# Reordering the opening of an attention-plus-Fourier kernel, and who copies its sums out of PSUM

## The chip, the cores and the metric

The kernel runs on one core of one Trainium2 chip. A core has a matrix engine (TensorE, "PE" in the profile; its weight loads are listed apart as "PEld"), a vector engine (VectorE, "DVE"), an activation engine (ScalarE, "ACT"), a general engine (GpSimd, "POOL") and a queue engine (SyncE, "SP"). Each runs its own list of instructions strictly in order and waits at semaphores for the others. Matrix results appear in PSUM, eight banks of 128 x 512 float32; operands lie in SBUF. DMA transfers are issued by an instruction on one of the engines' queues (here SP, ACT or POOL).

The metric is the device time of one execution in microseconds, the median of several runs. Less is better.

## The reference

Inputs are one sequence of 2048 rows of width 512 and fixed weights. What is computed, in float32:

```python
x = A_x                                                   # 1 x 2048 x 512
g = sigmoid((x * gate_w).sum(-1, keepdims=True))
qkv = x @ wqkv                                            # 32 heads of 16
p = softmax(q @ k.T * 16 ** -0.5)                         # per head, 2048 x 2048
a = (p @ v) @ wo
b = dft_seq_re @ (x @ dft_hid_re.T) - dft_seq_im @ (x @ dft_hid_im.T)
out = g * a + (1 - g) * b
```

`wqkv` and `wo` are scaled by 64, so the scores are large and the softmax needs the maximum of each row of scores subtracted.

## The kernel before

**Arithmetic.** TensorE takes rounded float32 operands ("F32R"). To keep precision, an operand is split into a rounded high part and the remainder: `split` (L369) is a copy on ScalarE (L370) and a subtraction on another engine (L371). A product is then three products: high x high, high x low, low x high.

**Two stages.** The program has a *front* and then *rounds*. The front computes q and k transposed (`project_t`, L432), v and the two hidden transforms (`project_s`, L464), and, beside them, a part of the *scans*. A scan is a first pass over the scores of two heads that finds each row's maximum. The rounds then do the scores proper, their exponentials on ScalarE, the sums of exponentials times values (`pv`, L671), the remaining scans, and the large sequence transform as filling (`fill`, L925).

**Slots in the front.** `products` (L351) issues one output tile: 12 pairs of operands, each as two half-height matmuls, one on the upper 64 rows of the array (L356) and, 17 pairs later, one on the lower 64 rows (`follow`, L340). 80 such tiles make 960 pairs. One pair is one *slot*: after each, `beside()` (L287) advances the counter `slots`, runs whatever `after(n, f)` (L263) made due n slots later, and, once `scan_at(FOLD_PACE)` has been called, issues scans at a spacing of 2.05 slots (`scan_folded`, L178). Each engine's program is the order in which these calls are made. Tile n uses PSUM bank n mod 3; `close` (L436) of tile n, run 28 slots after the tile's first slot, empties it by a ScalarE copy (L445, `eh`) and a VectorE subtraction (L446, `el`) and, for the first two groups of k, another ScalarE copy (L448). The parts are then stored to DRAM from SyncE's queue (L458).

**The start.** SyncE loads, in pieces, the transposed x (four column parts c, four row parts d, into `raws[0..3]`), and the columns of `wqkv` for q and k (`rq`, `rk`), each in a `near` and a `far` half. Meanwhile TensorE does `NWARM` transposes of an identity (L505). The splits of x part 0 and of the near half of `wq` are made at once, the others at slots given in L509 to L514. Tiles follow the `order` of L515: q and k of group 0 and q of group 1 for part 0, then k and q of group 0 for parts 1 to 3, then the other groups of q, then k.

**Scans in the front.** There are 64 scans for each pair p of heads, 368 (`FRONT`) in the front: pairs 0 to 4 and 48 scans of pair 5. In the front a scan handles folded keys: for each scan one ScalarE instruction (L190) reads one bank and one VectorE instruction (L192) another. The rows of q and folded keys for a pair are four tiles (`PARTS`: k0, k1, q0, q1) of four loads each, issued by `load_scan_beside` (L277), for pair 0 on SyncE's queue, for the others on ScalarE's. Twelve SBUF slots of 128 x 1024 (`stk0` to `stk11`), taken as a ring by `piece` (L102), hold raw weights, raw x and all such row tiles. Near the end of the front the rows for the rounds are loaded too: `used[0]` (28 loads) and `first_rows` (12 loads), both in one go on SyncE's queue.

**Folding the keys.** `fold_keys` (L416) takes a difference of two parts of k on GpSimd, splits it and stores it to `kf_d`; it is started 3 slots after the odd part's tile is closed.

**Quotients.** In the rounds the sums of exponentials times values of two heads and two halves of 1024 queries share one PSUM tile, `pvb`. After every 16 steps `quotients` (L705) copies `pvb` to SBUF tile `ob`. From macro round 42 on (`SINGLES`) ScalarE copies columns 0 to 255 (L710) and VectorE columns 256 to 511 (L711) of the same tile. The order of scores, scans and filling in a round is a table (`ORDERS`, L47); banks are chosen by a planner (`Banks`, L612) at build time.

## Time and profile before

| | |
|---|---|
| median of 3 runs | 1731.57 us (1730.52 to 1739.37) |
| profiled execution, its own time | 1734.79 us |
| its span, first to last instruction | 1732.8 us |
| mean granted TensorE clock | 0.994 |
| PE busy | 1708.2 us (99%) |
| DVE busy | 1249.2 us (72%) |
| ACT busy | 1358.7 us (78%) |
| POOL busy | 687.7 us (40%) |
| front, first product to last scan | 5.8 to 344.0 us |
| scans outside the front | 351.6 to 1595.5 us |

Times in profile rows count from the span's start. A row of the table of stretches has the stretch, its length, then busy time and number of instructions of each engine (of one source line alone where the text says so), the granted clock, the DMA engines' share and GB/s. A row of the timeline has start, duration, engine, line, operation, tiles and shapes; in brackets stands how long the engine was idle before and what ended that. A row of waits has who waited for whom, the sum in us, how often, and the longest. PE is counted busy where its pipeline still holds a matmul, so that small stalls show as a lower count of matmuls in a stretch and not as idle time.

### The profile page before, as it was taken

The page shows a single profiled execution, that of the slowest core. Times are in us where ns is not written, and L with a number is a line of the kernel's source. Part 1 is how long each engine was busy: PE and PEld are TensorE (multiplying, and loading weights), DVE is VectorE, ACT ScalarE, POOL GpSimd, SP SyncE. Part 2 cuts the span into 40 slices and gives each one's busy share as a digit, 9 for nine tenths or more (in the row PEclk, how much of TensorE's full clock was granted, in tenths as well). Part 3 has the DMA queues.
Part 4 walks back from the last instruction along what each step waited for, and adds up shares of the span by engine and source line. Part 5 has one row for each costly group of instructions (what it writes and reads, how often), then busy time and mean ns, then how long its engine had stood idle before and what let it go on. Part 6 is the DMA issues. An engine that isn't in the chain of part 4 may idle for free.

```text
span 1732.8 us, 36968 instructions
## 1 busy us (share of the span) xinstructions
PE 1708.2 (99%) x13657; PEld 1026.9 (59%) x13657; DVE 1249.2 (72%) x2385; ACT 1358.7 (78%) x2615; POOL 687.7 (40%) x860
## 2 busy tenths in 40 slices
PE   8999999999999999999999999999999999999998
PEld 6777778744435555555555555555555555555554
DVE  5589899866667777777777777777777777777434
ACT  5589988789997777777777777777777777777785
POOL 0254301344564544444444434434443443443121
PEclk9999999999999999999999999999999999999999
DMA  7575233564443333232333257333332422425522
GB/s 262 198 234 170 72 117 121 185 188 131 112 149 94 94 87 90 80 102 70 88 83 95 64 155 229 102 89 103 97 87 82 126 78 76 122 82 154 147 55 100
DMA packets 140004, 206.59 MB, mean 119 GB/s; under 512 B 58848, under 2 KB 61392, under 8 KB 139824
## 3 DMA queue, kind: packets, MB, share of 16 engines
q1 hardware_dynamic: 94992, 167.46, 31.5%
q0 software_dynamic: 41056, 27.86, 6.1%
q10 hardware_dynamic: 3776, 8.92, 1.9%
q8 instruction: 107, 1.75, 0.4%
q14 instruction: 73, 0.60, 0.1%
HBM read 137.89 MB, written 65.81 MB: 118 GB/s over the span
## 4 chain that ended last, share of the span: by engine, by line
PE 88%; DMA 4%; POOL 2%; issue 2%; DVE 1%; ACT 1%; SPq 0%; ACTq 0%; DVEq 0%; POOLq 0%
PE pvb L675 25%; PE z L920 21%; PE s L696 15%; PE s L665 12%; PE xy L340 5%; PE s L186 5%; PE xy L356 4%; DMA bs_d<-ol 1%; DMA o_d<-ol 1%; DMA wraw<-wqkv 0%; POOL ol L964 0%; ACT fold L190 0%; DVE y L865 0%; POOL el L275 0%; DMA lc<-ob 0%
## 5 line engine op out<-in xcount | busy, mean ns | idle before, releaser
L655 ACT ACTIVATE e<-s 128x512 f32<-128x512 f32 x2048 | 1073.4, 648 | 256.6 <-PE s L665 224.7
L698 DVE TENSOR_REDUCE mx<-s 128x1 f32<-128x512 f32 x1312 | 850.6, 687 | 284.3 <-PE s L665 194.9
L665 PE MATMUL s<-qs,ks 50*128 50x512 f32 x2048 | 656.7, 423 | 0.0
L675 PE MATMUL pvb<-e,va 128*17 128x512 f32 x4096 | 497.9, 596 | 0.0
L696 PE MATMUL s<-ks,qs 48*128 48x512 f32 x1312 | 487.9, 419 | 1.8 <-DVE mx L698 1.4
L920 PE MATMUL z<-b,chi 64*128 64x512 f32 x2060 | 471.9, 392 | 0.0
L665 PEld LDWEIGHTS s<-qs,ks 50*128 50x128 f32 x2048 | 338.7, 184 | 133.9 <-ACT e L655 110.4
L696 PEld LDWEIGHTS s<-ks,qs 48*128 48x128 f32 x1312 | 218.1, 185 | 197.4 <-issue 116.5
L920 PE MATMUL z<-b,clo 64*128 64x512 f32 x1030 | 300.9, 392 | 0.0
L920 PEld LDWEIGHTS z<-b,chi 64*128 64x128 f32 x2060 | 281.7, 186 | 27.4 <-issue 0.8
L192 DVE CUSTOM_DVE_ANT_0 fold<-s,fold 128x512 f32<-128x512 f32 x368 | 242.7, 689 | 32.9 <-ACT fold L190 14.2
L186 PE MATMUL s<-ks,qs 48*128 48x512 f32 x736 | 237.8, 404 | 5.6 <-ACT fold L190 5.3
L244 POOL CAST chi<-craw 128x512 fp32r<-128x512 f32 x126 | 77.3, 613 | 385.8 <-PE z L920 377.2
L190 ACT ACTIVATE fold<-s 128x512 f32<-128x512 f32 x368 | 203.1, 604 | 33.5 <-PE s L186 29.1
L675 PEld LDWEIGHTS pvb<-e,va 128*17 128x17 f32 x4096 | 90.1, 96 | 213.4 <-issue 212.2
L245 POOL TENSOR_TENSOR clo<-craw,chi 128x512 fp32r<-128x512 f32 x126 | 161.8, 1284 | 10.5
L920 PEld LDWEIGHTS z<-b,clo 64*128 64x128 f32 x1030 | 157.1, 186 | 13.6
L186 PEld LDWEIGHTS s<-ks,qs 48*128 48x128 f32 x736 | 135.8, 186 | 43.8 <-ACT fold L190 17.0
L714 POOL DMA_DIRECT2D lc<-ob x124 | 63.1, 515 | 230.1 <-DVE ob L711 211.0
L356 PE MATMUL xy<-w,b 64*128 64x512 f32 x384 | 121.9, 402 | 0.0
L340 PE MATMUL xy<-w,b 64*128 64x512 f32 x384 | 117.9, 395 | 0.0
L865 DVE SCALAR_TENSOR_TENSOR y<-z,g,y 128x512 f32<-128x512 f32 x44 | 32.5, 750 | 64.6 <-PE z L920 63.0
(130 smaller groups left out, 1509.5 us busy)
## 6 DMA issues: line engine op xcount, KB each, us to landing
craw<-cr SPq DMA_DIRECT2D x64, 256.0 KB
craw<-ci SPq DMA_DIRECT2D x64, 256.0 KB
qs<-q_d SPq DMA_DIRECT2D x110, 128.0 KB
ks<-k_d SPq DMA_DIRECT2D x108, 128.0 KB
ab_d<-ab SPq DMA_DIRECT2D x32, 256.0 KB
y_d<-y SPq DMA_DIRECT2D x32, 256.0 KB
b<-bs_d SPq DMA_DIRECT2D x32, 256.0 KB
o_d<-oh POOLq DMA_DIRECT2D x28, 256.0 KB, 9.6
```

Source lines behind the costliest of these rows:

```text
L186: nc.tensor.matmul(ps, rows.q[qb // 8][b:b + 48, qb % 8 * P:(qb % 8 + 1) * P], rows.k[c // 2][b:b + 48, c % 2 * 512:(c % 2 + 1) * 512], st ...
L190: seen_by(nc.scalar.activation(fold[j], ps, AF.Relu))
L192: seen_by(nc.vector.tensor_tensor_reduce(out=fold[j], in0=ps, in1=fold[j], scale=1.0, scalar=-3.0e38, op0=ALU.add, op1=ALU.max, accum_out= ...
L245: sub(lo, raw, hi.bitcast(F32))
L340: ins = nc.tensor.matmul(ps, lhs[64:P], rhs[64:P], start=False, stop=last)
L356: nc.tensor.matmul(ps, lhs[0:64], rhs[0:64], start=n == 0, stop=False)
L655: nc.scalar.activation(e, ps, AF.Exp, scale=SCALE)
L665: nc.tensor.matmul(ps, rows.k[kb // 8][b:b + 50, kb % 8 * P:(kb % 8 + 1) * P], rows.q[h][b:b + 50, c * 512:c * 512 + 512], start=True, sto ...
L675: nc.tensor.matmul(pvb[r:r + VC, :], va[:, kb, 2 * p + j, :], es[step][c, j][0], start=kb == 0, stop=kb == NB - 1, tile_position=(0, r))
L696: nc.tensor.matmul(ps, rows.q[qb // 8][b:b + 48, qb % 8 * P:(qb % 8 + 1) * P], rows.k[c // 2][b:b + 48, c % 2 * 512:(c % 2 + 1) * 512], st ...
L698: nc.vector.tensor_reduce(mx[p][:, j, qb, c:c + 1], ps, axis=AX.X, op=ALU.max)
L920: nc.tensor.matmul(ps, pr_.lhs(j), pr_.rhs(j), start=group.count[j] == 1, stop=group.count[j] == group.size)
```

## The change

Two groups of edits.

In the front:

- `NWARM` goes from 20 to 32 transposes, and three further groups of six transposes (`fillers`) are put after the third, sixth and ninth pair of the first tile.
- The slots at which operands are split move: x parts 1, 2 and 3 start at slots 10, 32 and 56 (before 18, 42 and 66); the far half of `wq` at 84 (before 52), the far half of `wk` at 124 with a spacing of 6 (before 76 with 4).
- The first `fold_keys` is started 36 slots after its tile is closed (before 3).
- The row tiles of pair 0 are loaded through GpSimd's queue (before SyncE's); those of the other pairs through SyncE's (before ScalarE's), beginning at scan 10 of pair 0 and scan 4 of the others (before 28 and 8), 5 slots apart (before 3).
- `used[0]` is loaded from scan 284 on, 5 slots between loads (before all at scan 312), and `first_rows` from scan 324 on, 3 slots between loads (before all at scan 334), into SBUF slots that are written out in `LAST_SLOTS` instead of the ring's next ones.

In the rounds:

- `quotients` copies all of `pvb` by one ScalarE instruction.

```diff
--- before.py
+++ after.py
@@ -35,10 +35,11 @@
 FRONT = 5 * SCANS + 48
 FOLDED = range(FRONT)
 FOLD_PACE = 2.05
-NWARM = 20
+NWARM = 32
 STEPS = NP * PERIODS
 MACROS = STEPS // 2
 LAG = 17
+LAST_SLOTS = ((6, 7, 0, 1), (8, 9, 10))
 SINGLES = 42
 EARLY = 0
 SPECTRAL = 8
@@ -94,14 +95,14 @@
 
 
         scanned, used, owner, next_slot = {}, {}, [None] * 12, [0]
-        HS = S // 2
+        HS, fixed = S // 2, []
 
         def free_slots():
             return [i for i in range(12) if owner[i] is None]
 
         def piece(dtype, name, who=None, ring=True):
 
-            i = next_slot[0] if ring else free_slots()[0]
+            i = fixed.pop(0) if fixed else next_slot[0] if ring else free_slots()[0]
             if ring:
                 next_slot[0] = (i + 1) % 12
             owner[i] = who
@@ -246,7 +247,7 @@
                 parts.append((hi, lo))
 
         seen, slots, due, count = [0], [0], [], [0]
-        first_rows = []
+        first_rows = Rows()
         pace = [None, 0.0]
         with ExitStack() as px:
             psf = px.enter_context(tc.tile_pool(name="psf", bufs=1, space=PSUM, reuse_waits="tile"))
@@ -277,9 +278,9 @@
             def load_scan_beside(p):
                 rows, loads = scanned.setdefault(p, Rows()), []
                 for part in PARTS:
-                    load_part(rows, None, p, part, nc.scalar if p else nc.sync, kf_d, True, loads.append)
+                    load_part(rows, None, p, part, nc.sync if p else nc.gpsimd, kf_d, True, loads.append)
                 for n, load in enumerate(loads):
-                    after((3 if p else 2) * n, load)
+                    after((5 if p else 2) * n, load)
 
             def scan_at(spacing):
                 pace[0] = spacing
@@ -294,17 +295,18 @@
                 while seen[0] < FRONT and pace[1] >= 1.0:
                     pace[1] -= 1.0
                     n = seen[0]
-                    if n % SCANS == (28 if n < SCANS else 8) and n - n % SCANS + SCANS < FRONT:
+                    if n % SCANS == (10 if n < SCANS else 4) and n - n % SCANS + SCANS < FRONT:
                         load_scan_beside(n // SCANS + 1)
-                    if n == FRONT - SCANS + 8:
-                        used[0] = Rows()
+                    if n in (FRONT - SCANS - 20, FRONT - SCANS + 20):
+                        loads = []
+                        fixed[:] = LAST_SLOTS[n > FRONT - SCANS]
                         for part in PARTS:
-                            load_part(used[0], "use", 0, part, nc.sync, k_d, True)
-                    if n == FRONT - SCANS + 30:
-                        first_rows.append(Rows())
-                        for part in PARTS:
-                            if part != "q0" or FRONT % SCANS < SCANS // 2:
-                                load_part(first_rows[0], "scan", FRONT // SCANS, part, nc.sync, k_d, True)
+                            if n < FRONT - SCANS:
+                                load_part(used.setdefault(0, Rows()), "use", 0, part, nc.sync, k_d, True, loads.append)
+                            elif part != "q0" or FRONT % SCANS < SCANS // 2:
+                                load_part(first_rows, "scan", FRONT // SCANS, part, nc.sync, k_d, True, loads.append)
+                        for k, load in enumerate(loads):
+                            after((5 if n < FRONT - SCANS else 3) * k, load)
                     scan_folded(n, 0, scan_bank)
                     done = behind(n - 1)
                     seen[0] += 1
@@ -346,7 +348,7 @@
                 if last:
                     close(ps)
 
-            starts = set()
+            starts, fillers = set(), []
 
             def products(parts, close):
 
@@ -364,6 +366,8 @@
                     behind_.append((ps, lhs, rhs, n == len(pairs) - 1, close))
                     if len(behind_) > LAG:
                         follow()
+                    if n % 3 == 2 and fillers:
+                        fillers.pop()(6)
                     beside()
 
             def split(hi, lo, raw, engine):
@@ -450,7 +454,7 @@
                             after(5, nc.gpsimd.tensor_copy, hi, s)
                             after(6, nc.gpsimd.tensor_sub, lo, s, hi.bitcast(F32))
                         if folded and c % 2:
-                            after(3, fold_keys, f, c - 1, even[0], s)
+                            after(36 if early and c == 1 else 3, fold_keys, f, c - 1, even[0], s)
                         after(9 if early else 12, store, 0, hi)
                         after(12 if early else 18, store, 1, lo)
 
@@ -501,17 +505,21 @@
                 after(40, nc.sync.dma_start, gb, gate.to_broadcast([P, D]))
 
                 warm = [scan_bank(), scan_bank()]
-                for n in range(NWARM):
-                    nc.tensor.transpose(warm[n % 2][:, 0:P], ident, ident)
+                def keep_warm(k):
+                    for n in range(k):
+                        nc.tensor.transpose(warm[n % 2][:, 0:P], ident, ident)
+
+                keep_warm(NWARM)
+                fillers.extend([keep_warm] * 3)
                 for d in range(ND):
                     split_x(d, 0)
                     split_w(wq, d, rq[d], cols=near)
                 for d in range(ND):
                     after(1 + 2 * d, split_w, wk, d, rk[d], nc.vector, near)
-                    after(52 + 4 * d, split_w, wq, d, rq[d], nc.vector, far)
-                    after(76 + 4 * d, split_w, wk, d, rk[d], nc.vector, far)
-                    for c in range(1, NC):
-                        after(24 * c - 6 + 4 * d, split_x, d, c)
+                    after(84 + 4 * d, split_w, wq, d, rq[d], nc.vector, far)
+                    after(124 + 6 * d, split_w, wk, d, rk[d], nc.vector, far)
+                    for c, at in zip(range(1, NC), (10, 32, 56)):
+                        after(at + 4 * d, split_x, d, c)
                 order = [(wq, q_d, 0, 0), (wk, k_d, 0, 0), (wq, q_d, 1, 0)]
                 order += [(w, dst, 0, c) for c in range(1, NC) for w, dst in ((wk, k_d), (wq, q_d))]
                 for n, (w, dst, f, c) in enumerate(order):
@@ -585,7 +593,7 @@
                 run_due(True)
 
         assert seen[0] == FRONT, seen
-        scanned[FRONT // SCANS] = first_rows[0]
+        scanned[FRONT // SCANS] = first_rows
 
         with ExitStack() as pa:
             psl = pa.enter_context(tc.tile_pool(name="psl", bufs=1, space=PSUM, reuse_waits="tile"))
@@ -707,8 +715,7 @@
                 if now[0] < SINGLES:
                     nc.vector.tensor_copy(ob, pvb)
                 else:
-                    nc.scalar.copy(ob[:, 0:256], pvb[:, 0:256])
-                    nc.vector.tensor_copy(ob[:, 256:512], pvb[:, 256:512])
+                    nc.scalar.copy(ob, pvb)
                 lc = sm.tile([P, 16], F32, tag="lc", name="lc")
                 for n, (c, j, r) in enumerate(quads):
                     nc.gpsimd.dma_start(lc[32 * n:32 * n + 32, :],
```

## The prediction

> **What bounds the kernel now.** The page comes first: how much of the span is TensorE's, and what the chain that ended last consists of.
>
> ```profile
> span 1732.8 us, 36968 instructions
> PE 88%; DMA 4%; POOL 2%; issue 2%; DVE 1%; ACT 1%; SPq 0%; ACTq 0%; DVEq 0%; POOLq 0%
> ```
>
> 88% of the chain is TensorE. So a time is won only where TensorE stands still or runs slowly, and 4% DMA and 2% "issue" in the chain say that such places exist. To find them I count products of the front (L356, one per slot) in stretches between the starts of output tiles. Columns: stretch, length, PE busy (count), PEld busy (count), granted clock, DMA share, GB/s.
>
> ```profile
> 5.81:16.43 10.62, 9.38 (x24) 6.42 (x25) 0.68 0.99 344
> 16.43:41.35 24.92, 21.26 (x85) 14.79 (x84) 1.00 0.66 243
> 48.07:50.95 2.88, 2.88 (x12) 2.14 (x13) 1.00 0.84 314
> 41.35:64.91 23.56, 21.05 (x85) 14.96 (x84) 1.00 0.74 255
> 90.23:102.86 12.63, 8.81 (x25) 4.94 (x24) 0.86 0.75 231
> 205.05:312.60 107.55, 95.44 (x301) 52.90 (x300) 1.00 0.34 106
> 312.60:324.74 12.14, 8.64 (x24) 5.20 (x25) 0.86 0.70 217
> ```
>
> A count one above a multiple of 12 is a product that only reaches into the stretch. Without scans a quiet tile takes 2.88 us, 0.240 us a slot (third row). With scans beside it, the long quiet stretch gives 107.55 / 300 = 0.3585 us a slot (sixth row). What the other rows have above these paces is what a better order could win:
>
> - 5.81 to 16.43: 10.62 - 24 x 0.240 = 4.86 us
> - 16.43 to 41.35: 24.92 - 84 x 0.240 = 4.76 us
> - 41.35 to 64.91: 23.56 - 84 x 0.240 = 3.40 us
> - 90.23 to 102.86: 12.63 - 24 x 0.3585 = 4.03 us
> - 312.60 to 324.74: 12.14 - 24 x 0.3585 = 3.54 us
>
> That is 20.6 us. The quiet pace with scans can't be bettered by this change, because VectorE holds it:
>
> ```profile
> L192 DVE CUSTOM_DVE_ANT_0 fold<-s,fold 128x512 f32<-128x512 f32 x147 | 96.6, 689 | 8.9 <-ACT fold L190 2.1 <-PE s L186 1.3 <-PE xy L340 0.4
> ```
>
> 147 such instructions in the stretch from 205.05 to 312 us are one in 0.73 us, each taking 0.689 us, and their number stays.
>
> **Part 1: the first two tiles (more transposes, earlier splits).** The clock by single microseconds, TensorE's timeline and the last operand of the first tile:
>
> ```profile
> 7.00:8.00 1.00, 0.46 (x3) 0.03 (x1) 0.00 (x0) 0.28 (x1) 0.00 (x0) 1.00 0.98 344
> 9.00:10.00 1.00, 1.00 (x3) 0.79 (x3) 1.00 (x3) 0.83 (x3) 0.00 (x0) 0.60 1.06 380
> ```
>
> ```profile
> 1.35 4.53 PE L505 MATMUL s<-ident 128*128 128x128 f32 x20 [1.35 <-POOL ident masks.py:199]
> 5.81 1.65 PE L356 MATMUL xy<-b,w 64*128 64x512 f32 x6
> 8.70 2.88 PE L356 MATMUL xy<-b,w 64*128 64x512 f32 x6 [1.24 <-ACT w L370]
> 10.01 0.42 DVE L371 TENSOR_TENSOR w<-raws,w 128x256 fp32r<-128x256 f32 x1
> ```
>
> TensorE runs dry at 7.46 us, waits 1.24 us for operands, and a clock of 0.60 from 9 to 10 us is half clock from 9.2 us on; the mean of 0.68 over 5.81 to 16.43 (0.32 x 10.62 / 0.5) makes that 6.8 us at half. The transposes cost 4.53 / 20 = 0.227 us each, and 12 + 18 = 30 are added. If each costs that and hides nothing, the second tile ends at 1.35 + 50 x 0.227 + 24 x 0.240 = 18.4 us instead of 16.43: +2.0. If they all fit into waits and keep the clock, the first tile can't end before its last operand, 10.43 us, plus three slots, and the second 12 slots later: 10.43 + 15 x 0.240 = 14.0 us, that is -2.4. The added transposes stand in TensorE's own queue ahead of products that are ready, so the truth is nearer the first end; some are covered by the 1.24 us wait. I take +1.0.
>
> The Trainium skill, "TensorE: Matmul & The Clock Gate" (Part 4), speaks against this edit: it says that a transpose on TensorE does not count as activity for the clock gate in the way a matmul does. By it the fillers would cost their time and not hold the clock. The trace doesn't bear that out so far: from 7 to 8 us, with little but transposes before, it is 1.00. What it would give is rival (b).
>
> **Part 2: splits by need and the later first fold (16.43 to 41.35).** In the timeline, a split's subtraction that takes 0.69 us alone takes far longer beside GpSimd's folding subtraction:
>
> ```profile
> 9.40 0.69 DVE L371 TENSOR_TENSOR b<-raws,b 128x512 fp32r<-128x512 f32 x1
> ...
> 32.15 1.29 POOL L275 TENSOR_TENSOR ke<-ke,fh 128x512 fp32r<-128x512 f32 x1 [1.08 <-ACT fh L275]
> 32.22 1.78 DVE L371 TENSOR_TENSOR b<-raws,b 128x512 fp32r<-128x512 f32 x1
> ```
>
> That is 1.1 us lost on VectorE, in whose queue the emptying of PSUM (L446) stands behind the splits; tiles 3 and on wait for a bank. The change puts the far halves of `wq` (8 instructions) and `wk` (8) behind all of x, and the fold 33 slots later, after the splits of x. Moving them costs nothing on the way: no instruction is added, and they are still 12 slots or more ahead of the tiles that read them. What stays is the emptying of the k tiles, three dependent copies of about 0.6 us within 8 slots (1.9 us), before three tiles of this stretch; at half a microsecond each that is 1.5 of the 4.76 us. I take -2.5, between 0 and -4.8.
>
> **Part 3: pair 0's rows through GpSimd (41.35 to 64.91).** Now SyncE issues them between the stores:
>
> ```profile
> L156 SPq DMA_DIRECT2D qs<-q_d x8: 418/430/509, 57.8 to 62.1; - x8
> ```
>
> ```profile
> ACT eh L445 <- DMA q_d<-eh: 3.1, 1, 3.1
> ```
>
> The last is issued at 62.1 us, one microsecond before the first scan, and stores behind them come so late that ScalarE waits 3.1 us for a free `eh`, so that PSUM is emptied late. On GpSimd's queue these 16 loads stand in nobody's way: its own work there is the second fold, over before slot 146. Their price, from other transfers on that queue (median ns to issue), and from issue to landing:
>
> ```profile
> L714 POOL DMA_DIRECT2D lc<-ob x124: 496/506/677, 389.5 to 1683.7; - x124
> L744 POOL DMA_DIRECT2D o_d<-oh x28: 858/875/887, 426.1 to 1583.0; - x28
> ```
>
> ```profile
> o_d<-oh POOLq DMA_DIRECT2D x28, 256.0 KB, 9.6
> ```
>
> The first scan, 42 slots or 10.1 us after the first load, needs the ninth and tenth load: 10 x 0.506 = 5.1 us plus half of 9.6 (half the bytes) lands at 9.9 us, in time; 10 x 0.875 + 4.8 = 13.6 us is 3.5 late. So between -3.4 and about +2 (3.5 late less part of the won 3.4). The loads write 32 or 16 rows like `lc`, so I stay near that end: -1.5.
>
> **Part 4: the other pairs' rows from ScalarE's to SyncE's queue.** The stall at 90 us, in the chain and in the waits:
>
> ```profile
> 87.38 8.50 DMA wraw<-wqkv
> ```
>
> ```profile
> ACT fold L190 <- DMA wraw<-wqkv: 1.9, 1, 1.9
> ```
>
> A weight transfer of 8.5 us holds up ScalarE, which has no use for it in a fold: one of the row loads in its queue waits, and the fold behind it. With the loads on SyncE that wait falls on stores and loads, and ScalarE, VectorE and TensorE run on as long as the store buffers last. Late next would be the stores, with three `eh` buffers, about two tiles of 4.3 us. Of 4.03 us I take -3.0 (0 to -4.0). The 80 moved issues are 80 instructions more for SyncE at 0.43 us (the row of `qs` above), 34 us over 280; spread at 5 slots (1.8 us) they cost +0.5, at worst +3 if stores queue behind them.
>
> **Part 5: the loads for the rounds, spread.** SyncE's timeline, first and last of the 28, and ScalarE behind them:
>
> ```profile
> 298.99 2.40 SPq L156 DMA_DIRECT2D ks<-k_d  x4
> ...
> 312.25 2.72 SPq L156 DMA_DIRECT2D qs<-m_d  x4
> ```
>
> ```profile
> 317.27 0.60 ACT L564 ACTIVATE ab<-xy 128x512 f32<-128x512 f32 x1 [2.21 <-DMA ab_d<-ab]
> ```
>
> SyncE is taken for 16 us; the store of `ab` comes after it, ScalarE waits 2.21 us for its buffer with folds queued behind, and TensorE loses 3.54 us. Five slots apart, a store waits for one load. The last is then issued some 50 slots (18 us) before the rounds, time enough for a landing of 9.6 us. I take -3.0 (0 to -3.5).
>
> **Part 6: the quotients.** One round, from one group of `pv` to the next and the one after:
>
> ```profile
> 557.33 1.91 PE L675 MATMUL pvb<-e,va 128*17 128x512 f32 x16
> ...
> 559.35 0.37 ACT L710 COPY ob<-pvb 128x256 f32<-128x256 f32 x1 [0.86 <-issue]
> ...
> 559.75 0.42 DVE L711 COPY ob<-pvb 128x256 f32<-128x256 f32 x1 [1.61 <-ACT ob L710]
> 560.09 3.98 DVE L698 TENSOR_REDUCE mx<-s 128x1 f32<-128x512 f32 x6
> ...
> 560.83 0.18 PEld L696 LDWEIGHTS s<-ks,qs 48*128 48x128 f32 x1 [0.43 <-DVE mx L698]
> ...
> 563.24 1.91 PE L675 MATMUL pvb<-e,va 128*17 128x512 f32 x16
> ...
> 568.85 0.62 PE L675 MATMUL pvb<-e,va 128*17 128x512 f32 x4
> ```
>
> The two copies are not parallel: VectorE's begins when ScalarE's has ended, and VectorE stands still 1.61 us for it. Its reductions then free PSUM banks late, and TensorE waits. The round with the copy takes 563.24 - 557.33 = 5.91 us, the next 568.85 - 563.24 = 5.61: 0.30 us. How often, and what ScalarE needs for a whole tile:
>
> ```profile
> L711 DVE COPY ob<-pvb x26: 424/425/426, 559.8 to 1681.4; 128x256 f32<-128x256 f32 x26
> ```
>
> ```profile
> L696 PE MATMUL s<-ks,qs x1312: 384/395/625, 351.6 to 1595.5; 48*128 48x512 f32 x188
> ```
>
> ```profile
> L448 ACT COPY s<-xy 128x512 f32<-128x512 f32 x18 | 10.5, 585 | 2.6 <-DVE el L446 1.5 <-PE xy L340 0.5 <-PE s L186 0.2
> ```
>
> 26 copies are (1681.4 - 559.8) / 25 = 44.9 us apart; 23 of them lie before the scans end at 1595.5, and only there has VectorE reductions to be late with. Without VectorE's copy: -23 x 0.30 = -6.9 us. Against it, ScalarE's copy grows from 0.372 to 0.585 us and shifts the first exponential after it by 0.21 us; if TensorE waits for all of that, 23 x 0.21 = 4.9 us come back. ScalarE has just idled 0.86 us there and the round leaves it gaps, so I take 0.4 of it: -6.5, between -2.0 and -7.5 (some rounds lose a little more than 0.30).
>
> **The sum.** +1.0 - 2.5 - 1.5 - 3.0 + 0.5 - 3.0 - 6.5 = -15.0 us. All good ends give -25, all bad ones +5. Against the profiled execution's own 1734.79 us that is 1719.8; it stood 3.2 above the median of the runs, and 1731.57 - 15 = 1716.6, so I forecast 1717. A measurement of this kernel can tell about 0.5% from no change, here 8.7 us: faster means below 1723, slower above 1740.
>
> **Rivals.**
>
> (a) *The front only moves its stalls.* SyncE gets 80 more loads and still must wait for weights. For it: the wait of 8.5 us does not go away, it changes its queue. Against it: SyncE's stores have buffers behind them and ScalarE's folds had none. Then only the quotients count: 1731.57 - 6.5 = 1725, no change that can be told.
>
> (b) *Transposes don't hold the clock.* The 6.8 us at half clock stay, of which 3.4 are lost, and the fillers are paid in full: 18.4 + 3.4 = 21.8 us for the second tile, +5.4 instead of +1.0. For it: the clock fell at 9 us in spite of 20 transposes. Against it: it fell after a gap in the products. Sum -10.6: 1721. (The rule that says so is in the Trainium skill, "TensorE: Matmul & The Clock Gate", Part 4.)
>
> (c) *Slower: SyncE becomes late with the rows of a pair.* TensorE takes scans in order, so a late tile stops it wholly. From scan 4 of one pair to scan 0 of the next are 60 scans of 0.73 us, 44 us; the 16 loads take 80 slots, 29 us. So it decides once SyncE's in-order waits add more than 15 us in one pair; to be slower by 8.7 us, five pairs must lose 24 us together, waits of some 20 us each. For it, SyncE already waits long for GpSimd:
>
> ```profile
> SPq L534 <- POOL xg L538: 37.5, 12, 8.9
> ```
>
> Against it: the longest is 8.9 us, below 15. It would give about 1742.
>
> **How the numbers follow.** Forecast 0.66, (a) 0.14, (b) 0.10, (c) 0.10. The forecast's own range is 1707 to 1724; the bad ends and (a) reach 1729, and with all good ends 1706.6, or a little below if a product tile gains above the quiet pace. From 1704 to 1730 leaves (c) and some of the tails out, 2 in 10. Faster: nearly all of the forecast (0.61), most of (b) (0.08) and a little of (a) (0.02), 0.71; slower: (c) and a tail, 0.11; the same: 0.18.
>
> **What would show it.** Right: rounds with a copy as long as their neighbours, 5.6 us, one ScalarE copy of 0.585 us and no VectorE wait beside it; 24 slots around the weight load in about 9.5 us instead of 12.6; no stretch below 1.00 clock at 98 and 320 us; first scan before 63 us. Wrong: `fold` waiting for DMA as before, TensorE waiting for `qs` or `ks`, a first tile that ends after 14 us at half clock, or a round where exponentials start late and the score's weight load waits for ScalarE.

## The result, and the profile after

The changed kernel takes 1719.03 us (median of 4 runs, 1718.58 to 1721.17) against 1731.85 us for the kernel before in the same comparison: a ratio of 0.992, with a 95% interval of 0.989 to 0.9949. The forecast was 1717, from 1704 to 1730. The profiled execution took 1718.87 us by its own time, close to the median, so what follows is its trace against the one of before, whose own time (1734.79 us) was 3.2 above its median: 15.7 us of span between the two profiles, 12.8 us between the medians.

The page of the changed kernel, its span and the chain that ended last, by engine:

```profile
span 1717.1 us, 37031 instructions
PE 89%; DMA 4%; POOL 2%; issue 1%; DVE 1%; ACT 1%; SPq 0%; DVEq 0%; POOLq 0%; ACTq 0%
```

TensorE's share of the chain rose by one point only, and DMA still has 4%. So stalls went, and something with DMA in it remains. The stretches say where. Products of the front (now L358), by the same tiles as in the prediction; columns are stretch, length, PE busy (count), PEld busy (count), granted clock, DMA share, GB/s:

```profile
6.99:15.76 8.77, 6.56 (x25) 4.08 (x25) 1.00 1.04 356
15.76:39.28 23.52, 20.99 (x85) 14.86 (x85) 1.00 0.67 245
39.28:62.81 23.53, 21.00 (x86) 15.14 (x85) 1.00 0.84 299
87.98:96.40 8.42, 7.54 (x25) 4.20 (x24) 1.00 0.75 261
198.60:305.57 106.97, 95.22 (x301) 53.08 (x300) 1.00 0.35 114
305.57:313.91 8.34, 7.50 (x24) 4.37 (x25) 1.00 0.62 180
```

Both stalls at the loads are gone (12.63 to 8.42, 12.14 to 8.34, now below 24 x 0.3585 = 8.60 us, the quiet pace that the prediction had taken as the best to be had), the second row won 1.40, the third nothing. The clock is 1.00 in all of them.

For the rounds I count the matmuls of `pv` (now L683), 128 of them to the 16 steps between two copies of `pvb`. Two such stretches with single rounds, and then 22 with scans and a ScalarE copy each:

```profile
440.17:471.53 31.36, 16.84 (x129) 2.12 (x129) 1.00 0.37 103
471.53:509.56 38.03, 17.70 (x128) 2.14 (x128) 0.91 0.43 120
555.62:1543.10 987.48, 336.33 (x2817) 64.73 (x2817) 1.00 0.34 100
```

The same last two stretches of the kernel before:

```profile
483.93:516.71 32.78, 16.85 (x129) 2.13 (x129) 1.00 0.48 143
563.24:1557.67 994.43, 336.34 (x2817) 64.78 (x2817) 1.00 0.34 99
```

The 22 copies gained 994.43 - 987.48 = 6.95 us, 0.32 each. But one stretch of 16 steps, the fifth of the rounds, takes 38.03 us where its neighbour takes 31.36 and the kernel before took 32.78. That is 5.25 us given back in one place, of which the prediction knew nothing. The whole account, profile against profile:

| stretch | before | after | difference |
|---|---|---|---|
| start to third tile | 16.43 | 15.76 | -0.67 |
| the next 7 tiles | 24.92 | 23.52 | -1.40 |
| the next 7 (rows of pair 0) | 23.56 | 23.53 | -0.03 |
| tiles 16 to 21 | 25.32 | 25.17 | -0.15 |
| tiles 22 and 23 (rows of pair 1) | 12.63 | 8.42 | -4.21 |
| 48 quiet tiles | 209.74 | 209.17 | -0.57 |
| tiles 72 and 73 (loads for the rounds) | 12.14 | 8.34 | -3.80 |
| to the first `pv` | 32.13 | 32.18 | +0.05 |
| single rounds, first four stretches | 127.06 | 125.44 | -1.62 |
| single rounds, fifth stretch | 32.78 | 38.03 | +5.25 |
| the stretch with the first scans | 46.53 | 46.06 | -0.47 |
| 22 stretches with scans | 994.43 | 987.48 | -6.95 |
| the end | 175.13 | 174.00 | -1.13 |
| sum | 1732.8 | 1717.1 | -15.7 |

What happens in the fifth stretch is in the chain of the changed kernel, followed from 468 to 489 us (start, duration, what):

```profile
468.36 6.50 DMA bs_d<-ol
...
474.99 1.27 POOL ol L971
476.27 1.08 POOL bs_d L973 x2
477.35 1.00 POOL lc L721 x2
...
478.83 5.28 DMA lc<-ob
...
484.39 0.25 DVE lc L728
484.64 0.56 DVE mx L706
485.20 0.04 issue
485.24 1.38 PE s L704 x2
```

Read it from below. TensorE waits for VectorE to free a bank (`mx`); VectorE stands at the reciprocal of the sums (`lc`, L728); that waits for four loads of 2 KB, of which the last takes 5.28 us to land; and GpSimd issued them late, at 477 us, because it stood itself at a 6.50 us store of the Fourier part (`bs_d<-ol`) whose buffer it needed. VectorE and TensorE show how long:

```profile
484.39 0.25 DVE L728 RECIPROCAL lc<-lc 128x16 f32<-128x16 f32 x1 [5.90 <-DMA lc<-ob]
485.24 1.38 PE L704 MATMUL s<-ks,qs 48*128 48x512 f32 x2 [4.40 <-DVE mx L706]
```

The mean clock of 0.91 in that stretch is 0.09 x 38.03 / 0.5 = 6.8 us at half clock. It begins inside the wait (483.3 to 490.2 us, where TensorE's wait ends at 485.24), so it costs less than half of that: 38.03 - 31.36 = 6.67 us are lost against the neighbour, 4.40 of them the wait and 2.3 the clock.

### The profile page after: what moved, and what is told of

Read it like the earlier page. It is cut to its first block, busy times and chain, and to the rows that moved or that the text cites. A ratio compares the mean times of both kernels' runs of the same rounds, so it can differ in the third digit from the quotient of the medians.

```text
span 1717.1 us, 37031 instructions
## 1 busy us (share of the span) xinstructions
PE 1696.4 (99%) x13687; PEld 1026.8 (60%) x13687; DVE 1239.5 (72%) x2359; ACT 1355.2 (79%) x2615; POOL 696.4 (41%) x876
## 4 chain that ended last, share of the span: by engine, by line
PE 89%; DMA 4%; POOL 2%; issue 1%; DVE 1%; ACT 1%; SPq 0%; DVEq 0%; POOLq 0%; ACTq 0%
PE pvb L683 25%; PE z L927 21%; PE s L704 15%; PE s L673 12%; PE xy L358 5%; PE xy L342 5%; PE s L187 5%; DMA o_d<-ol 1%; DMA bs_d<-ol 1%; DMA lc<-ob 1%; POOL ol L971 0%; DMA q_d<-el 0%; POOL lc L721 0%; DVE y L872 0%; DMA bs_d<-oh 0%
## 5 line engine op out<-in xcount | busy, mean ns | idle before, releaser
L673 PE MATMUL s<-qs,ks 50*128 50x512 f32 x2048 | 647.4, 421 | 0.0
L683 PE MATMUL pvb<-e,va 128*17 128x512 f32 x4096 | 497.8, 596 | 0.0
L683 PEld LDWEIGHTS pvb<-e,va 128*17 128x17 f32 x4096 | 90.0, 96 | 210.6 <-issue 209.3
L358 PE MATMUL xy<-w,b 64*128 64x512 f32 x384 | 121.0, 399 | 0.0
```

The costliest lines, as they stand in the source:

```text
L358: nc.tensor.matmul(ps, lhs[0:64], rhs[0:64], start=n == 0, stop=False)
L673: nc.tensor.matmul(ps, rows.k[kb // 8][b:b + 50, kb % 8 * P:(kb % 8 + 1) * P], rows.q[h][b:b + 50, c * 512:c * 512 + 512], start=True, sto ...
L683: nc.tensor.matmul(pvb[r:r + VC, :], va[:, kb, 2 * p + j, :], es[step][c, j][0], start=kb == 0, stop=kb == NB - 1, tile_position=(0, r))
```

## The experiments

Unless said otherwise each is an edit of the changed kernel. Ratios are against the kernel before on the same chip. Where there was one run, only its stretches are read.

**The two groups apart.** In `e1_quotients_only` the kernel before gets the quotients' edit alone, in `e2_front_only` the changed kernel gets the old quotients back.

```diff
 # e1_quotients_only, on the kernel before
-                    nc.scalar.copy(ob[:, 0:256], pvb[:, 0:256])
-                    nc.vector.tensor_copy(ob[:, 256:512], pvb[:, 256:512])
+                    nc.scalar.copy(ob, pvb)
 # e2_front_only, on the changed kernel: the same lines the other way round
```

> The kernel before with only the last edit: ScalarE alone copies the sums in rounds. If VectorE's wait for ScalarE's half is what made a round with a copy long, all 23 such rounds that still have scans become as long as their neighbours: 23 x 0.32 = 7.4 us, about 1724.4 us against 1731.9, ratio 0.9957. If ScalarE's longer copy only moves the wait to the exponentials, they keep 0.2 us and about 1729 comes out. If the long wait of 5.7 us in the changed kernel's single rounds (479 to 487 us) comes from this edit, it shows here too, with 38 us instead of 32.8 for the fifth period of 16 steps; I expect it not to.

> The changed kernel with the sums copied by both engines again. If the two groups of edits add up, 1719.0 + 7.4 = 1726.4 us, and the rounds with a copy have 5.04 + 0.87 us again where the others have 4.73 + 0.87. The first group of sums starts at 346.1 us as in the changed kernel (356.9 before). The fifth period of 16 steps has its wait of 5.7 us if that comes from the front, and takes 38 us; if it comes from the copy, 32.8.

Measured: 1726.84 us (6 runs), ratio 0.9953 [0.9938, 0.9968], and 1727.48 us (6 runs), ratio 0.9957 [0.994, 0.9974]. The two together, 0.991, agree with the whole change's 0.992. The 22 stretches with scans, `e1_quotients_only` first and then `e2_front_only`:

```profile
560.28:1548.03 987.75, 336.33 (x2816) 64.77 (x2816) 1.00 0.35 100
```

```profile
553.21:1547.13 993.92, 336.33 (x2817) 64.75 (x2817) 1.00 0.35 99
```

The first is that of the changed kernel, the second that of the kernel before: -6.7 us belong to the copy alone. The fifth stretch of single rounds took 32.15 and 32.56 us, so neither half of the change by itself sets it to 38.

The first of the two has the front of the kernel before, and shows that front a second time. Its rows for the two bursts of loads:

```profile
89.49:99.77 10.28, 7.69 (x26) 4.24 (x24) 1.00 0.82 268
310.97:321.55 10.58, 7.51 (x25) 4.37 (x25) 1.00 0.72 228
```

The stalls are there, but the clock did not fall behind them, as it did in the profile of before (0.86 in both). So of the 4.21 and 3.80 us above, 1.9 and 2.2 us are the stalls themselves. Most of the rest is a clock that falls in some executions and not in others: 0.14 of 12.63 and of 12.14 us below full is 3.4 to 3.5 us at half clock each time, which costs up to 1.7. This is one reason why the profiles differ by more than the medians. The second stall also varies where its loads are spread: the eleven executions of that kind took 8.28 to 9.31 us for tiles 72 and 73, and the profile of the changed kernel is near the low end.

**A later reciprocal.** The three steps after a copy (reciprocal, spreading, scaling) are staged 3, 6 and 9 macro rounds later; here in the single rounds 5, 8 and 11.

```diff
 # e3_late_reciprocal
-                    for n, f in zip((3, 6, 9) if m < SINGLES else ...
+                    for n, f in zip((5, 8, 11) if m < SINGLES else ...
```

> The changed kernel with the three steps of the quotients in single rounds 5, 8 and 11 macro rounds after the sums instead of 3, 6 and 9. Theory: the wait at 479 to 487 us is VectorE's reciprocal, in order ahead of the scans' reductions, waiting for a transfer that GpSimd issued late; two macro rounds (7.8 us) later it has landed, the fifth period takes 31.4 us instead of 38.0, and the time falls by 5.7 to 7 us, to about 1712.5. Rival: the SyncE loads of that moment are what TensorE lacks; then the wait stays and 1719 comes out.

Measured: 1713.92 us (4 runs, 1712.89 to 1714.55), ratio 0.9877 [0.9858, 0.9896]. The fifth stretch of single rounds, and the chain of the whole span by engine:

```profile
472.45:503.81 31.36, 16.85 (x129) 2.13 (x129) 1.00 0.45 133
```

```profile
PE 94%; DMA 1%; DVE 1%; ACT 1%; issue 1%; POOL 0%; DVEq 0%; ACTq 0%
```

The loads of `lc` are issued as late as in the changed kernel (477.3 to 480.0 us), but the reciprocal, at 487.2 us, no longer waits for them. The chain's 4% of DMA fell to 1%, and its 2% of GpSimd to nothing: it now runs nearly past GpSimd and its transfers. These shares are not the gain, since 3% of the span is 51 us; the gain is in the stretch (38.03 to 31.36 us) and in the time (1713.92 us).

**Fewer transposes.** 20 again, and none between the products. The transposes compute nothing that is used.

```diff
 # e4_few_transposes
-NWARM = 32
+NWARM = 20
-                fillers.extend([keep_warm] * 3)
```

> The changed kernel with 20 transposes at the start and none between the first products. If the transposes hold the clock gate open, the clock falls to half at about 9 us for 3.4 to 6.8 us as before, the third tile starts at 16 to 16.5 us instead of 15.8, and the total is 0 to 1 us longer. If transposes do not count for the gate, the clock stays as it is with them, and the third tile starts 2 to 3 us earlier (some 13.3 us), as their time is saved.

Measured: one run, 1718.74 us. The first two tiles (products alone), and one microsecond near their end with all five engines (PE, PEld, DVE, ACT, POOL):

```profile
5.81:16.88 11.07, 10.03 (x24) 6.61 (x25) 0.71 1.02 346
16.00:17.00 1.00, 1.00 (x8) 0.80 (x6) 0.00 (x0) 0.00 (x0) 0.00 (x0) 0.50 1.07 372
```

Without the added transposes the products begin 1.18 us earlier and the third tile 1.12 us later, since 6.8 us run at half clock (from 10.4 to 17.2 us). So the transposes do hold the clock.

The other executions say the same: in the three without the added ones (this run, the kernel before and `e1_quotients_only`) the clock opened at 5.0 to 6.95 us and fell 3.4 us later each time, for 6.8 us; in the eleven with them it opened at 4.1 to 7.3 us and did not fall in these tiles. From the first product to the third tile that is 8.76 to 8.78 us in all eleven, and 11.07, 10.62 and 10.41 without. What is left after their own cost is less sure than the 1.12 us here, since the first product came anywhere from 6.31 to 7.87 us in the eleven and the third tile from 15.08 to 16.64 (without them: 15.85 to 16.88). Whether the twelve at the start or the eighteen between the products do it was not separated. The transposes are not seen in the total, because this run's fifth stretch took 34.67 us instead of 38.03.

**The rows of pair 0 on SyncE's queue again.**

```diff
 # e5_rows0_sync
-                    load_part(rows, None, p, part, nc.sync if p else nc.gpsimd, kf_d, True, loads.append)
+                    load_part(rows, None, p, part, nc.sync if p else nc.sync, kf_d, True, loads.append)
```

> The changed kernel with pair 0's rows issued by SyncE again (2 slots apart, as before). In the changed kernel the seven tiles from 9 to 16 take 23.5 us, no less than before (23.6), though SyncE was freed: a store there takes 6.9 us to land while the DMA engines are full from 52 to 58 us. If the 16 transfers themselves fill the DMA engines whichever queue issues them, the stretch stays at 23.5 give or take 0.7. If GpSimd's queue was a gain that something else hid, it grows by 1.5 us or more; if its dense issue (0.5 us each) is the harm, it falls to 22.

Measured: one run, 1714.2 us; its fifth stretch was 31.36 us, so the total says nothing about pair 0. The stretch of seven tiles:

```profile
39.10:63.75 24.65, 21.02 (x85) 14.96 (x84) 1.00 0.82 277
```

That is 1.1 us more than with GpSimd's queue. But nine executions of kernels in which nothing of this part differs took 23.1 to 25.8 us there, so one look can't carry it: inconclusive.

**The rows of the other pairs: queue or times?** The change moved them from ScalarE's queue to SyncE's, and also earlier and further apart. First the queue undone and the times kept, then the times undone and the queue kept.

```diff
 # e6_rows_scalar
-                    load_part(rows, None, p, part, nc.sync if p else nc.gpsimd, kf_d, True, loads.append)
+                    load_part(rows, None, p, part, nc.scalar if p else nc.gpsimd, kf_d, True, loads.append)
 # e9_old_times
-                    after((5 if p else 2) * n, load)
+                    after((3 if p else 2) * n, load)
-                    if n % SCANS == (10 if n < SCANS else 4) and ...
+                    if n % SCANS == (28 if n < SCANS else 8) and ...
```

> The changed kernel with the other pairs' rows issued by ScalarE again, at the new times and spacing. Tiles 22 to 24 took 12.6 us before and take 8.4 in the changed kernel. If the queue is the cause (a row load waiting in ScalarE's queue behind the weight transfer), they take 11 to 12.6 us again; if the earlier start and wider spacing are, they stay at 8.4 to 9, and the total within 1 us of 1719.

> The changed kernel with the other pairs' rows on SyncE's queue, but at the old times: from scan 28 of pair 0 and scan 8 of the others, 3 slots apart. With the loads on ScalarE at the new times the wait at tiles 22 and 23 was gone (8.47 us). If the move of the queue would also have done alone, they take 8.4 to 9 us here; if it is the times alone, a row load behind the weight transfer now holds up SyncE's stores and 10 to 12 us come out.

Measured: one run each, 1717.96 and 1713.92 us. Tiles 22 and 23 of the first and of the second:

```profile
90.31:98.78 8.47, 7.58 (x25) 4.39 (x24) 1.00 0.79 290
```

```profile
86.84:95.25 8.41, 7.53 (x25) 4.28 (x24) 1.00 0.88 293
```

Both are as good as the whole change (8.42). Either edit is enough by itself: in neither does a fold wait for a DMA any more, be it that ScalarE's loads are issued at another time or that they left its queue. In `e9_old_times` the wait for the weight transfer is still there, 3.1 us in two waits between 60 and 345 us, but SyncE bears it. No run takes back both and keeps the rest of the change, so that one of the two is needed rests on the kernel before and on `e1_quotients_only`, where both, and the rest of the front, are old. And 80 more issues on SyncE cost nothing that the stretch shows.

**The loads for the rounds in one go again**, at scans 284 and 324.

```diff
 # e7_burst
-                            after((5 if n < FRONT - SCANS else 3) * k, load)
+                            after(0, load)
```

> The changed kernel with the 28 loads of the first rounds in one go at scan 284 and the 12 others in one go at scan 324, in the new SBUF slots. If SyncE's burst is what held up the stores and stopped TensorE, 3 to 4 us come back in the tiles from 64 to 68 and 1 to 2 in those around 71 to 74, first sums at 350 to 352 instead of 346. If waiting for occupied SBUF slots was the cause, both stretches stay at 4.2 to 4.3 us a tile.

Measured: one run, 1720.34 us. The 24 slots behind the burst of 28, and the same slots of the changed kernel:

```profile
283.69:297.70 14.01, 8.94 (x25) 4.84 (x24) 0.88 0.55 174
```

```profile
283.90:292.68 8.78, 7.79 (x25) 4.09 (x24) 1.00 0.47 153
```

5.23 us more, of which up to 1.7 are clock (0.12 x 14.01 / 0.5 = 3.4 us at half): the burst of 28 is the cause of the stall, wherever it stands, and spreading it removes it. The burst of 12 shows nothing clear. It was issued at 305.0 to 312.5 us, and tiles 72 and 73 took 9.35 us, where executions with spread loads took up to 9.31; the 1 to 2 us that were expected there did not come out.

**VectorE alone copies the sums.**

```diff
 # e8_vector_alone
-                    nc.scalar.copy(ob, pvb)
+                    nc.vector.tensor_copy(ob, pvb)
```

> The changed kernel with VectorE alone copying the sums in rounds. If what cost 0.32 us a round was that reductions started late for whatever reason, VectorE's own copy of 0.69 us, started when the sums end, still ends only 0.2 us earlier than the two copies did: rounds with a copy stay 0.1 to 0.2 us longer than 4.73 + 0.87, 3 to 5 us in all, about 1722 to 1724. If only the wait for ScalarE was harmful, they are as short as with ScalarE alone and 1719 comes out.

Measured: one run, 1719.64 us; 22 stretches with scans:

```profile
550.93:1542.95 992.02, 336.35 (x2816) 64.78 (x2817) 1.00 0.35 100
```

4.54 us more than with ScalarE (987.48), 0.21 a copy, and still 2.4 us less than both engines together (994.43). So it is VectorE's time, copying or waiting, that counts there, and splitting the copy was the worst of the three.

**The old order of splits, and the old first fold.**

```diff
 # e10_old_splits
-                            after(36 if early and c == 1 else 3, fold_keys, f, c - 1, even[0], s)
+                            after(3, fold_keys, f, c - 1, even[0], s)
-                    after(84 + 4 * d, ...); after(124 + 6 * d, ...); x parts at (10, 32, 56)
+                    after(52 + 4 * d, ...); after(76 + 4 * d, ...); x parts at (18, 42, 66)
```

> The changed kernel with the old slots of the splits and the first fold 3 slots after its tile. Tiles 2 to 9 took 24.9 us before and 23.5 in the changed kernel. If the order of the splits and the fold made that difference, tiles 5 and 6 take 5 us for one of them again and the stretch 24.5 to 25.5; if it came from SyncE's or the clock's side, it stays near 23.5. A subtraction of a split beside GpSimd's folding subtraction takes 1.7 us again instead of 0.7.

Measured: one run, 1718.7 us. The second to the ninth tile, and the collision in its timeline:

```profile
15.69:40.65 24.96, 21.30 (x86) 14.79 (x85) 1.00 0.69 253
31.44 1.29 POOL L276 TENSOR_TENSOR ke<-ke,fh 128x512 fp32r<-128x512 f32 x1 [1.08 <-ACT fh L276]
31.49 1.78 DVE L375 TENSOR_TENSOR b<-raws,b 128x512 fp32r<-128x512 f32 x1
```

The old length (24.92) and the old collision are back, 1.44 us over the changed kernel. The three executions with the old order took 24.92 to 24.96 us, the eleven with the new one 22.68 to 23.78, so this difference stands clear of chance. It lies in one tile: tile 6, counted from 0, took 5.24 us in all three and 3.51 to 3.54 in all eleven. How much belongs to the splits and how much to the later fold was not separated. VectorE's subtraction ends 0.54 us after GpSimd's. In the changed kernel the first subtraction of the fold still meets a split, and the same holds:

```profile
29.35 1.30 POOL L276 TENSOR_TENSOR ke<-ke,s 128x512 f32<-128x512 f32 x1 [27.10 <-ACT s L452]
...
29.82 1.38 DVE L375 TENSOR_TENSOR b<-raws,b 128x512 fp32r<-128x512 f32 x1 [1.17 <-ACT b L374]
```

VectorE ends at 31.20, 0.55 us after GpSimd's end at 30.65. The Trainium skill, "SBUF — State Buffer" (Who interferes with whom), says that a VectorE instruction with two SBUF inputs contends with a GpSimd instruction that reads SBUF; both rows agree with that. The second subtraction of the fold, moved to 39.09 us, meets none.

**Both repairs, and the change again beside it.** The reciprocal as in `e3_late_reciprocal`, and pair 0's rows begun 14 slots earlier and 3 slots apart; on the same chip the changed kernel itself.

```diff
 # e11_both (e12_after_again has no edit)
-                    after((5 if p else 2) * n, load)
+                    after((5 if p else 3) * n, load)
-                after(38, load_scan_beside, 0)
+                after(24, load_scan_beside, 0)
-                    for n, f in zip((3, 6, 9) if m < SINGLES else ...
+                    for n, f in zip((5, 8, 11) if m < SINGLES else ...
```

> The changed kernel with the later reciprocals (5, 8, 11 macro rounds) and pair 0's loads on GpSimd begun 14 slots earlier and 3 slots apart instead of 2. If the dense loads fill the DMA engines and hold up a store, tile 13's 4.5 us fall to 3 to 3.5 and tiles 9 to 16 from 23.5 to 22.5; the first scan is not later. With the 5.7 us of the reciprocal about 1712.5 us, ratio 0.987. If the transfers' bytes alone decide, 23.5 stays and the time is that of the later reciprocals alone, 1713.9.

> The changed kernel once more, beside the one above on the same chip. If the wait at the reciprocal is a fixed part of it, the fifth period takes 38 us in this profile too and the median is 5 to 7 us above the run above; if its length is chance, it lies between 31.4 and 38 and the runs spread by several us.

Measured: 1714.23 us (4 runs, 1712.96 to 1715.45), ratio 0.9873 [0.9853, 0.9893], against 1718.53 us (4 runs, 1715.97 to 1721.63), ratio 0.9897 [0.9875, 0.9918]. The runs of the two do not overlap, and 4.3 us lie between the medians. The rows of pair 0 gained nothing by it; seven tiles of `e11_both`:

```profile
38.87:62.40 23.53, 21.16 (x85) 15.13 (x85) 1.00 0.86 298
```

23.53 us as in the changed kernel. Here tile 14 is the long one (4.27 us) and tile 13 is not (3.16), but so it is in `e2_front_only` and `e4_few_transposes`, which lack this edit. So what the stretches show of the gain is the reciprocal's. In the second profile of the changed kernel the fifth stretch took 35.78 us, not 38.03. Over all kernels that keep the steps 3, 6 and 9, its length follows the reciprocal's wait for `lc` closely, if not exactly, from whatever it comes:

| kernel | wait, us | stretch, us |
|---|---|---|
| changed kernel | 5.90 | 38.03 |
| e12_after_again | 4.03 | 35.78 |
| e4_few_transposes | 2.93 | 34.67 |
| e8_vector_alone | 2.62 | 34.36 |
| before | 2.52 | 32.78 |
| e7_burst | 2.14 | 32.41 |
| e1_quotients_only | 1.88 | 32.15 |
| e10_old_splits | 1.87 | 32.18 |
| e6_rows_scalar | 1.75 | 32.35 |
| e2_front_only | 1.41 | 32.56 |
| e5_rows0_sync | 0.34 | 31.36 |
| e9_old_times | 0 | 31.37 |

The wait of 0.34 us cost nothing. In the four executions with 2.62 us or more the clock fell as well (0.95 in `e4_few_transposes`, `e8_vector_alone` and `e12_after_again`, 0.91 in the changed kernel), in the others not. The profile of the changed kernel is the worst of the twelve.

## Why the prediction was right, and where its steps were not

The time, 1719.03, lies 2 us from the forecast, in the range and on the side that was given 0.71. The sum of -15.0 us against the profile of before came out as -15.7. But the terms behind it differ more than the sum does, and that they add up is in part luck: the stretches that the six parts speak of gained 17.1 us together, those of which nothing was said gained 3.9 (1.6 of it in the first four single stretches, where the clock had fallen once in the profile of before), and 5.25 came back in a place that was not in the sum.

- **Part 1, +1.0 forecast: -0.67.** The term was mis-sized, at its unit price. 0.227 us for a transpose came from 20 of them, which stand 0.213 us apart to the last, as at half clock: in the changed kernel they start 0.213 us apart until 5.5 us and 0.109 us apart after it. The 32 took 5.70 us, 1.17 more than the 20, and a group of six between products takes 0.87 us, 0.145 each:

```profile
1.36 5.70 PE L510 MATMUL s<-ident 128*128 128x128 f32 x32 [1.36 <-POOL ident masks.py:199]
6.99 0.96 PE L358 MATMUL xy<-b,w 64*128 64x512 f32 x3
7.88 0.87 PE L510 MATMUL s<-ident 128*128 128x128 f32 x6
```

  And they kept the clock: 1.00 at the place where it had been 0.60 (columns after the length: PE, PEld, DVE, ACT and POOL busy, clock, DMA share, GB/s; so too in the stretches of Part 3).

```profile
9.00:10.00 1.00, 1.00 (x7) 0.61 (x6) 1.00 (x3) 0.83 (x3) 0.00 (x0) 1.00 1.06 402
```

  Rival (b) is refuted by the change and by `e4_few_transposes`, which has the half clock that it speaks of and lacks just the added transposes. The Trainium skill, "TensorE: Matmul & The Clock Gate" (Part 4), says that a transpose does not count as activity for the gate; for the transposes of this kernel the trace disagrees (clock 1.00 above, 0.50 without them), as far as they are of the kind that the page means.

- **Part 2, -2.5 forecast: -1.4.** Mechanism right (the collision with the fold comes back in `e10_old_splits`, and with it 1.7 us in tile 6), size too large. What I left to the emptying of the k tiles was 1.5 of 4.76 us; more than that stayed, since all seven tiles together still stand 23.52 - 84 x 0.240 = 3.4 us above the quiet pace. The fold's first subtraction, which still meets a split, is a part of it (1.38 us instead of 0.69); the rest was not taken apart.

- **Part 3, -1.5 forecast: 0.** This step failed. I had said that on GpSimd's queue the loads "stand in nobody's way". On GpSimd's queue they don't; but the store that frees `el` lands late while their data move. Timeline, chain and two stretches of the changed kernel:

```profile
55.85 0.69 DVE L450 TENSOR_TENSOR el<-xy,eh 128x512 fp32r<-128x512 f32 x1 [3.72 <-DMA q_d<-el]
```

```profile
48.86 6.90 DMA q_d<-el
```

```profile
52.00:54.00 2.00, 1.95 (x16) 1.61 (x18) 0.13 (x2) 0.48 (x1) 0.98 (x2) 1.00 1.08 349
54.00:56.00 2.00, 1.08 (x11) 0.75 (x7) 0.15 (x1) 0.11 (x1) 0.67 (x2) 1.00 1.01 332
```

  The store takes 6.90 us to land while the DMA engines are full (share 1.0 from 52 to 56 us), VectorE waits 3.72 us, and TensorE issues 11 matmuls in two microseconds instead of 16. The wait of 3.1 us that went (`eh`) was replaced by one of 3.7 (`el`). A wait for `el` stood in the trace of before as well (2.6 us), and the prediction priced the one for `eh` alone. That the full DMA engines are what delays the store is read from the two coming together; no run had less to move there. Whether SyncE's queue would cost 1.1 us more stays open (`e5_rows0_sync`); earlier issue does not help (`e11_both`).

- **Parts 4 and 5, -3.0 + 0.5 and -3.0 forecast: -4.2 and -3.8** by the two profiles; 1.9 and 2.2 of it are the stalls, most of the rest is clock that fell behind them in the profile of before. The cause of Part 4 was told one-sidedly: not the queue alone but the meeting of queue and time, and undoing either meeting point is enough. The +0.5 for SyncE's issues is not seen. Rivals (a) and (c) are refuted for this kernel: TensorE lost nothing in the 48 quiet tiles that follow (209.74 to 209.17 us), as it would behind late stores or late rows, and the front by itself (`e2_front_only`) is worth 7.4 us by the medians (ratio 0.9957, interval below 1), where (a) gave it nothing.

- **Part 6, -6.5 forecast: -6.95 in 22 copies,** -6.7 by `e1_quotients_only` and -6.4 by `e2_front_only` (993.92 against 987.48). I had let 0.4 us come back for ScalarE's longer copy; nothing comes back. One round with the copy, and the next group of `pv`:

```profile
550.03 1.91 PE L683 MATMUL pvb<-e,va 128*17 128x512 f32 x16
552.05 0.59 ACT L718 COPY ob<-pvb 128x512 f32<-128x512 f32 x1 [0.84 <-issue]
...
555.62 1.91 PE L683 MATMUL pvb<-e,va 128*17 128x512 f32 x16
...
561.23 1.05 PE L683 MATMUL pvb<-e,va 128*17 128x512 f32 x8
```

  It takes 5.59 us, the next 5.61: ScalarE had the gap.

- **What was not in the sum: +5.25.** The reciprocal in the single rounds. It stood in the trace of before with 2.52 us of waiting, and I had not asked what lay behind the front at all, though the rows of Parts 3 to 5 change what the DMA engines do. That the change makes it longer is not shown: four executions with its whole front had 1.41 to 5.90 us of it, two with the old front 1.88 and 2.52. What is shown is that it is worth 4 to 5 us to the changed kernel, by the medians, and can be taken away.

A better kernel than both is therefore the changed one with the reciprocal two macro rounds later: 1713.92 us, ratio 0.9877. Whether the same edit helps the kernel before was not tried.

## What to carry to other kernels

Loads that stand in an engine's queue should neither precede work that others wait for nor come in a burst: here spreading them removed one stall, and moving either their time or their queue removed another, but another queue was no help in Part 3, where the DMA engines were full. When two engines share a copy, look whether the second begins before the first ends; where it does not, as here, let the engine with the gap do all of it and measure. And before adding up the terms of a change, read the waits of the stages that it does not touch: a small load whose issuer and whose landing both vary by some microseconds is a stall in waiting, and more distance between it and its user cost nothing here.

## What the runs showed of the hardware

- A 2 KB load took 5.28 us from issue to landing among loads of 64 and 128 KB, where the median of the transfers to and from `lc` over the kernel is 2.2 us.
- After a stall of TensorE the granted clock is half for about 3.4 or 6.8 us, or not at all, for the same code: tiles 22 and 23 of the old front ran at 0.86 in one profile and at 1.00 in another, and the first stretch of the rounds took 31.36 us in the first profile of the changed kernel and 33.24 in the second. In these two places that went with 2.4 and 1.9 us.
- In the changed kernel the clock opened at 5.5 us, before any product had run (the first is at 6.99 us) and with nothing but transposes on TensorE. Over the fourteen executions it opened at 4.1 to 7.3 us. Whether these run in the array's own transpose mode is not in the trace, where they read as matmuls against an identity.
